# Fused attention and MLP on one core: batch 1's queries and keys loaded partly ahead of w_out, its scores started earlier, remainders and warm-up matmuls moved

## The chip, the cores and the metric

The kernel runs on one core of a Trainium2 chip. The core has five engines that run side by side and synchronise by semaphores: TensorE (PE in the profile; its weight loads are listed as PEld), VectorE (DVE), ScalarE (ACT), GpSimd (POOL) and SyncE (SP). Here GpSimd issues all loads, SyncE issues all stores and the transposing DMAs, and 16 DMA engines carry them all.

The metric is the device time of one execution in microseconds (us); the median of several runs is compared.

## The reference

Eight batches of causal attention with eight heads each, 576 positions and head size 64, with a decaying bias, are followed by a two-layer MLP with an exact GELU over all 4608 tokens:

```python
scores = scale * q @ k.T                          # per batch and head, 576 x 576
cum    = cumsum(maximum(s, 0))
scores = where(causal, -1e9, scores + minimum(-(cum_i - cum_j), 0))
attn   = softmax(scores)                          # with 1e-9 on the sum
x      = (attn @ v) as [4608 tokens, 512]
g      = gelu_exact(x @ w_in)                     # 512 -> 2048
out    = g @ w_out                                # 2048 -> 512, float32
```

## The kernel before, in words

**The attention.** One batch is treated as four pairs of heads (p = 0 to 3). For a pair, `sc_item` (L370) computes the scores with the key position on the partitions, in two units of up to 512 columns into PSUM tiles of the tag "sc" (two of them), and ScalarE takes the exponential into the tile P (L392, four buffers, one for each pair). `mask_item` (L398) zeroes the part above the diagonal on VectorE; for some pairs of batch 0 a matmul adds a large negative number instead (`neg=True`, L384). The decay is not added to the scores: each key position has a weight wb, v is multiplied by it once (`scale_v`, L225, L230, giving vv), and the numerator (lhsT = vv) and the denominator (lhsT = wb broadcast) come from two sets of matmuls (`av_mm`, L410, L414). `norm` (L427) takes the logarithm of the denominator and its negative exponential on ScalarE (L431, L432) and multiplies on VectorE into xT (L447), which is the MLP's input, transposed.

A batch has 576 positions and a PSUM bank holds 512 numbers of 4 bytes, so `av_item` (L452) does positions 0 to 511, and the last 64 positions of all four pairs, the remainder, share one bank (tile avr, `av_rest`, L467) and are normalised once (`norm_rest`, L473). Other than the "sc" tiles there are four PSUM banks: three of the tag "av", one of "mlp". An accumulator "wide" takes an "sc" tile.

**The MLP.** The 4608 tokens are cut into nine chunks of 512 (c). `l1_item` (L482) computes two of 16 tiles of the hidden layer (four matmuls of 128x128 by 128x512 for each, L495) and ScalarE applies GELU into gT (L501, L504). `l2_item` (L506) computes 128 tokens of the output (sub = 0 to 3) as 16 accumulating matmuls, ft = 0 to 15 (L514), which may be called in parts; after the last one VectorE copies the bank to o_sb (L521) and SyncE stores it (L523). Quarter i of w_out serves ft = 4i to 4i+3. A chunk's layer 1 has 64 matmuls, its layer 2 also 64.

**The order.** All engines follow the program's order (a manual schedule): each engine executes its own instructions in the order in which the program gives them, and waits where an operand or a buffer isn't ready. So the order of the calls in L563 to L719 is the plan. Batch 0's attention runs first (L563 to L600). In chunk c the layer 1 runs without other matmuls, and the attention of batch c+1 is mixed into its layer 2, since a chunk of 512 tokens needs the outputs of one batch more. Chunk 0 has its own order (L626 to L678), chunks 1 to 6 share one (L679 to L709).

Batches 0 and 1 have their q and k transposed on TensorE: `tr_item` (L353) does 18 small transposes into an "av" bank and a copy to qkT (L364; VectorE, or ScalarE where named). From batch 2 on, `interleave` (L174, L178) reorders on VectorE, `write_rows` (L185, L187) writes the rows to DRAM through SyncE's queue, and `transpose_rows` (L192, L194) reads them back with eight transposing DMAs, in the same queue.

**The loads.** GpSimd issues them in program order: first q, k and v of batch 0 and w_in, then, behind a small copy that waits for w_in's first quarter (`pace`, L593), the four quarters of w_out (L595, L247), q and k of batch 1 (`load_qk`, L596, four loads by `load_early`, L96, L101: the first q and k loads hold pairs 0 and 1, the second ones pairs 2 and 3), v of batch 1 (five loads, `load_v`, L196, L202) and q, k of batch 2. An issue waits when the load eight before it hasn't landed.

**Warm-up matmuls.** `keep_busy(n)` (L559, L561) issues n matmuls of 128x128 by 128x512 on zeros, whose result nobody reads.

**Side work.** `absmax` (L211) and `absmax_v` (L217) find the largest magnitudes for a check at the end, on VectorE, inside layer 1; when the check fails, a slow general version runs (from L724, not taken here).

Of the kernel before, what the change touches and what calls it, by code (L numbers as in the profile page):

```python
# [19 lines left out]
def kernel(  # L20
# [10 lines left out]
    nc = tc.nc  # L31
# [135 lines left out]
    def load_qk(b):  # L167
        for p in (0, 2):
            for n in "qk":
                load_early(b, n, p)  # L170
# [296 lines left out]
    def av_rest(b, p):  # L467
        if p == 0:
            rest_of[b] = ps.tile([128, 2, NP, SL], fp32, tag="av", bufs=3, name="avr")
        for den in range(2):  # L470
            av_mm(b, p, rest_of[b][:, den, p], [(jt, 0, n, off) for jt, n, off in REST], den)
# [87 lines left out]
    def keep_busy(n):  # L559
        for _ in range(n):  # L560
            nc.tensor.matmul(warm, lhsT=busy[:, :128], rhs=busy, start=True, stop=True)  # L561
# [10 lines left out]
    tr_item(0, 1, 1)  # L572
    nc.vector.tensor_scalar(neg_bf, tri_bf, 2048.0, -2048.0, op0=MULT, op1=ALU.add)
    weights_pe()
    keep_busy(2)
    sc_item(0, 1, neg=True)
    mask_item(0, 0, 0, nc.vector)
    mask_item(0, 0, 1, nc.vector)
    tr_item(0, 2, 0)
    tr_item(0, 2, 1)  # L580
    tr_item(0, 3, 0, nc.scalar.copy)
    tr_item(0, 3, 1)
    sc_item(0, 2, neg=True)
    keep_busy(1)
    sc_item(0, 3, neg=True)
    keep_busy(3)
    for st in range(ST - 1):
        scale_v(0, STS[st : st + 1], nc.vector)
    nc.vector.tensor_copy(uptri, tri_bf)
    nc.gpsimd.memset(amv, 0.0)  # L590
    nc.gpsimd.memset(ones, 1.0)
    nc.gpsimd.memset(qkT[1][:, 1, :, S:640], 0.0)
    nc.gpsimd.tensor_copy(pace, w_in_r[:, 0, 0:1])  # L593
    for i in range(4):
        load_w(1, i)  # L595
    load_qk(1)  # L596
    load_v(1)
    load_qk(2)
    for p in range(NP):
# [3 lines left out]
    for c in range(NCH):  # L603
# [9 lines left out]
            absmax_v(nb)  # L613
        if c == 0:
            absmax_v(0)
        if c < B:
            for p in range(NP):
                absmax(c, p)
# [7 lines left out]
        if c == 0:  # L626
            exp_set()
            load_v(2)
            l2_item(c, 0, av=True)
            scale_v(0, STS[ST - 1 :], nc.vector)  # L630
            for p in range(NP):
                av_rest(0, p)
            norm_rest(0)
            l2_item(c, 1, 0, 8)
            for p in (0, 1):
                for i in range(2):
                    tr_item(1, p, i)
            l2_item(c, 1, 8, 12)
            for i in range(2):
                tr_item(1, 2, i)  # L640
            l2_item(c, 1, 12)
            for i in range(2):
                tr_item(1, 3, i)
            sc_item(1, 0)
            l2_item(c, 2, 0, 6, av=True)
            sc_item(1, 1)
            l2_item(c, 2, 6, 12, av=True)
            scale_pair(1, 0)
            sc_item(1, 2)
            l2_item(c, 2, 12, av=True)  # L650
            sc_item(1, 3)
            scale_pair(1, 1)
            l2_item(c, 3, 0, 4)
            interleave(2, "q")
            write_rows(2, 0, nc.sync)
            av_item(1, 0, rest=False)
            scale_pair(1, 2)
            scale_pair(1, 3)
            l2_item(c, 3, 4, 8)
            interleave(2, "k")  # L660
            write_rows(2, 1, nc.sync)
            av_item(1, 1, wide=True, rest=False)
            l2_item(c, 3, 8, 12)
            for p in (0, 1):
                transpose_rows(2, p)
            av_rest(1, 0)
            av_rest(1, 1)
            av_item(1, 2, wide=True)
            l2_item(c, 3, 12)
            av_item(1, 3)  # L670
            norm_rest(1)
            gelu_set()
            for p in (2, 3):
                transpose_rows(2, p)
# [4 lines left out]
        elif nb < B:  # L679
            exp_set()  # L680
            l2_item(c, 0, 0, 4)
            sc_item(nb, 0)
            l2_item(c, 0, 4)
            late = int(c == 1)
            for p in range(1, NP):
# [185 lines left out]
```

## Time and profile before

| quantity | value |
|---|---|
| median of 5 runs | 333.86 us (333.38 to 335.44) |
| the profiled execution's own time | 333.19 us |
| span of the profile (first to last instruction) | 331.4 us |
| TensorE busy | 320.4 us, 97% of the span |
| VectorE, ScalarE, GpSimd busy | 193.4, 202.7, 65.0 us |
| TensorE's granted clock, mean | 0.997 |
| first layer-2 matmul of chunk 0 | 34.70 us |
| first layer-1 matmul of chunk 1 | 62.00 us |

How to read the profile: the page gives each engine's busy time, then the span in 40 slices of 8.3 us with a digit for the busy tenths of each. A line of a timeline or of the chain of waits has a start, a length, and the engine, line and tile of what ran; x16 means that 16 instructions are merged. In square brackets stands how long the engine had been idle just before, and, after the arrow, what ended that. Lengths of matmuls overlap, so the pace is read from the starts.

### The profile page before, as it was taken

The numbers are of one execution on the slowest core, as the hardware profiler recorded it, in microseconds if no ns is written. First come the engines' busy times: TensorE is split into PE (matmuls) and PEld (weight loads), VectorE is DVE, ScalarE is ACT, GpSimd is POOL, SyncE is SP. The second block draws the span as 40 slices with busy tenths as digits, with TensorE's granted clock in tenths as the row PEclk, the third lists the DMA queues.
The fourth block names the chain that finished last, engine by engine and source line by source line (L and its number), as shares of the span: only waits on it lengthen the run. The fifth ranks groups of instructions, "written<-read, shape, count | busy, mean of one in ns | idle before, by whom it ended". The sixth has DMA issues, their size and how long they took to land.

```text
span 331.4 us, 6416 instructions
## 1 busy us (share of the span) xinstructions
PE 320.4 (97%) x2590; PEld 163.8 (49%) x2590; DVE 193.4 (58%) x383; ACT 202.7 (61%) x288; POOL 65.0 (20%) x100
## 2 busy tenths in 40 slices
PE   8899899999999999999999999999999999999992
PEld 4554454545554455445544554455545544444452
DVE  6757187996569464947395657745693654150021
ACT  4886528868576766777576767677659566204400
POOL 8753351007000910620043002200000000000000
PEclk9999999999999999999999999999999999999998
DMA  7999999777965999899779465626600110010012
GB/s 121 222 211 208 219 228 242 203 135 110 276 199 132 156 227 267 171 199 270 156 145 206 139 189 127 138 105 166 132 15 32 45 53 2 32 63 32 3 63 71
DMA packets 53828, 47.30 MB, mean 143 GB/s; under 512 B 31328, under 2 KB 43872, under 8 KB 53792
## 3 DMA queue, kind: packets, MB, share of 16 engines
q0 software_dynamic: 15936, 23.07, 37.7%
q1 hardware_dynamic: 37856, 23.75, 27.0%
q8 instruction: 22, 0.36, 0.4%
q14 instruction: 14, 0.11, 0.1%
HBM read 36.85 MB, written 16.52 MB: 161 GB/s over the span
## 4 chain that ended last, share of the span: by engine, by line
PE 94%; ACT 3%; DVE 2%; issue 0%
PE h_ps L495 38%; PE o_ps L514 37%; PE sc_ps L376 5%; PE avn L414 4%; PE avd L414 3%; ACT P L392 2%; PE warm L561 2%; PE tr_ps L359 1%; PE avr L414 1%; PE o_ps L533 1%; DVE qkT L364 1%; PE avw L414 1%; PE sc_ps L384 0%; ACT ln L432 0%; ACT ln L431 0%
## 5 line engine op out<-in xcount | busy, mean ns | idle before, releaser
L514 PE MATMUL o_ps<-w_out_r,gT 128*128 128x512 bf16 x560 | 129.7, 380 | 0.0
L495 PE MATMUL h_ps<-xT,w_in_r 128*128 128x512 bf16 x576 | 126.0, 379 | 0.7 <-DVE xT L447 0.7
L495 PEld LDWEIGHTS <-w_in_r 128*128 128x128 bf16 x576 | 56.2, 98 | 68.7 <-issue 1.4
L501 ACT ACTIVATE gT<-h_ps 128x1024 bf16<-128x1024 f32 x54 | 54.3, 1022 | 48.8 <-PE h_ps L495 48.8
L392 ACT ACTIVATE P<-sc_ps 128x1024 bf16<-128x1024 f32 x64 | 61.9, 1021 | 33.8 <-PE sc_ps L376 32.2
L514 PEld LDWEIGHTS <-gT 128*128 128x128 bf16 x560 | 51.4, 98 | 58.6
L521 DVE COPY o_sb<-o_ps 128x512 f32<-128x512 f32 x35 | 24.1, 688 | 53.0 <-PE o_ps L514 53.0
L401 DVE TENSOR_TENSOR P<-P,tri_bf 128x512 bf16<-128x512 bf16 x58 | 24.3, 424 | 38.8 <-ACT P L392 38.6
L213 DVE TENSOR_REDUCE amx<-qkT 128x2 f32<-128x1152 bf16 x32 | 40.9, 1335 | 0.0
L447 DVE SCALAR_TENSOR_TENSOR xT<-avn,ln 128x256 bf16<-128x256 f32 (+3 forms) x64 | 21.7, 385 | 25.9 <-ACT ln L432 25.9
L202 POOL DMA_DIRECT2D raw_v<-in_v_dram x40 | 34.3, 882 | 10.1 <-DMA w_out_r<-in_moe_w_out_dram 6.5
L230 DVE TENSOR_TENSOR vv<-raw_v,wb 128x512 bf16<-128x512 f32 (+2 forms) x43 | 25.4, 644 | 0.9 <-DMA raw_v<-in_v_dram 0.9
L431 ACT ACTIVATE ln<-avd 128x256 f32<-128x256 f32 x56 | 18.6, 391 | 11.2 <-PE avd L414 11.2
L432 ACT ACTIVATE ln<-ln 128x512 f32<-128x512 f32 (+1 forms) x40 | 23.5, 587 | 1.3
L220 DVE TENSOR_REDUCE amv<-raw_v 128x1 f32<-128x2048 f32 (+1 forms) x16 | 23.0, 1470 | 1.4 <-DMA raw_v<-in_v_dram 1.4
L504 ACT ACTIVATE gT<-h_ps 128x512 bf16<-128x512 f32 x36 | 19.6, 603 | 6.3 <-PE h_ps L495 6.3
L376 PE MATMUL sc_ps<-qkT 64*128 64x256 bf16 (+2 forms) x320 | 21.5, 250 | 1.3 <-ACT P L392 0.9
L376 PEld LDWEIGHTS <-qkT 64*128 64x128 bf16 x320 | 13.2, 94 | 16.8 <-issue 14.2
L414 PEld LDWEIGHTS <-vv 128*64 128x64 bf16 x384 | 16.8, 109 | 8.3 <-issue 3.8
L414 PEld LDWEIGHTS <-wb 128*64 128x64 bf16 x384 | 17.0, 111 | 0.0
L414 PE MATMUL avn<-P,vv 128*64 128x256 bf16 x224 | 16.0, 265 | 0.0
L414 PE MATMUL avd<-P,wb 128*64 128x256 bf16 x224 | 15.4, 259 | 0.0
(94 smaller groups left out, 159.6 us busy)
## 6 DMA issues: line engine op xcount, KB each, us to landing
out_dram<-o_sb SPq DMA_DIRECT2D x35, 256.0 KB, 2.3
raw_v<-in_v_dram POOLq DMA_DIRECT2D x32, 256.0 KB, 7.4
rows<-qk_bf SPq DMA_DIRECT2D x12, 576.0 KB, 3.8
early_q<-in_q_dram POOLq DMA_DIRECT2D x14, 288.0 KB, 9.2
early_k<-in_k_dram POOLq DMA_DIRECT2D x14, 288.0 KB, 9.3
w_in_r<-in_moe_w_in_dram POOLq DMA_DIRECT2D x4, 512.0 KB, 11.0
w_out_r<-in_moe_w_out_dram POOLq DMA_DIRECT2D x4, 512.0 KB, 12.9
raw_v<-in_v_dram POOLq DMA_DIRECT2D x8, 128.0 KB, 9.3
```

Of the source, the lines that this page charges most:

```text
L202: nc.gpsimd.dma_start(out=t[:n_st, st, :, :], in_=bass.AP(tensor=v.tensor, offset=v.offset + b * H * S * D + st * 128 * D, ap=[[D, n_st], ...
L213: nc.vector.tensor_reduce(amx[:, b * NP + p], qkT[b % 2][:, :, p, :S], axis=AX, op=ALU.max, apply_absolute_value=True)
L230: eng.tensor_tensor(vb[:n_st, st0:st1, h0:h1, :], t[:n_st, st0:st1, h0:h1, :], wb[:n_st, st0:st1, b * H + h0 : b * H + h1] .unsqueeze(3).t ...
L376: nc.tensor.matmul(s_ps[:, e, off : off + n], lhsT=qkT[b % 2][e * 64 : e * 64 + 64, 1, p, jt * 128 : jt * 128 + 128], rhs=qkT[b % 2][e * 6 ...
L392: nc.scalar.activation(P[:, :, UO[u] : UO[u] + UW[u]], s_ps[:, :, : UW[u]], func=AF.Exp, scale=scale)
L401: eng.tensor_tensor(d, d, tri_bf.unsqueeze(1).unsqueeze(1).to_broadcast([128, 2, 2, 128]), op=MULT)
L414: nc.tensor.matmul(out[e * 64 : e * 64 + 64, lo : lo + n], lhsT=(wb[:, jt, b * H + h : b * H + h + 1].to_broadcast([128, 64]) if den else ...
L432: nc.scalar.activation(ln[:, :w], ln[:, :w], func=AF.Exp, scale=-1.0)
L495: nc.tensor.matmul(h_of[c, f2][i], lhsT=w_in_r[:, ko, ft * 128 : (ft + 1) * 128], rhs=xT[:, ko, c * NB % XW : c * NB % XW + NB], start=(ko ...
L501: nc.scalar.activation(gT_of[c][:, f2 * 2 : f2 * 2 + 2, :], hh_of[c, f2], func=AF.Gelu)
L514: nc.tensor.matmul(o_ps, lhsT=gT[:, ft, sub * 128 : (sub + 1) * 128], rhs=w_out_r[:, ft, :], start=(ft == 0), stop=(ft == FT - 1),)
L521: nc.vector.tensor_copy(o_sb, o_ps)
```

## The change

It has seven parts.

1. Batch 0's opening: `tr_item(0, 2, 0)` takes the place of `keep_busy(2)` ahead of the second pair's scores, and `tr_item(0, 2, 1)` stands ahead of the masks instead of behind them. `keep_busy(3)` behind the last scores is gone.
2. The scaling of v's fourth slice (positions 384 to 511) of batch 0 is cut into two halves of four heads.
3. The scaling of v's last slice (positions 512 to 575) of batch 0 is issued in chunk 0's layer 1, behind `absmax_v(0)` and ahead of `absmax`, instead of behind item 0 of layer 2.
4. The loads of the first halves of q and k of batch 1 are issued ahead of w_out's four quarters, the second halves behind them.
5. Layer 2 of chunk 0 opens with batch 0's remainder and the first transposes of batch 1, and every item of it is cut in two halves of 8 matmuls with transposes, scores and outputs of batch 1 in between. Items 0 and 2 and 3 use the "mlp" bank, item 1 an "av" bank (before: 0 and 2 "av", 1 and 3 "mlp").
6. Batch 1's remainder and its normalisation leave chunk 0's layer 2 and go into chunk 1's, ahead of and behind the first scores of batch 2.
7. All eight transposing DMAs of batch 2 now stand behind both writes of rows and the fourth store.

```diff
     weights_pe()
-    keep_busy(2)
+    tr_item(0, 2, 0)
     sc_item(0, 1, neg=True)
+    tr_item(0, 2, 1)
     mask_item(0, 0, 0, nc.vector)
     mask_item(0, 0, 1, nc.vector)
-    tr_item(0, 2, 0)
-    tr_item(0, 2, 1)
...
     sc_item(0, 3, neg=True)
-    keep_busy(3)
-    for st in range(ST - 1):
+    for st in range(ST - 2):
         scale_v(0, STS[st : st + 1], nc.vector)
+    for h in (0, H // 2):
+        scale_v(0, STS[ST - 2 : ST - 1], nc.vector, h, h + H // 2)
...
+    for n in "qk":
+        load_early(1, n, 0)
     for i in range(4):
         load_w(1, i)
-    load_qk(1)
+    for n in "qk":
+        load_early(1, n, 2)
     load_v(1)
     load_qk(2)
...
             absmax_v(0)
+            scale_v(0, STS[ST - 1 :], nc.vector)
...
             load_v(2)
-            l2_item(c, 0, av=True)
-            scale_v(0, STS[ST - 1 :], nc.vector)
             for p in range(NP):
                 av_rest(0, p)
+            tr_item(1, 0, 0)
+            tr_item(1, 0, 1)
+            l2_item(c, 0, 0, 8)
+            tr_item(1, 1, 0)
+            tr_item(1, 1, 1)
             norm_rest(0)
-            l2_item(c, 1, 0, 8)
-            for p in (0, 1):
-                for i in range(2):
-                    tr_item(1, p, i)
-            l2_item(c, 1, 8, 12)
-            for i in range(2):
-                tr_item(1, 2, i)
-            l2_item(c, 1, 12)
-            for i in range(2):
-                tr_item(1, 3, i)
             sc_item(1, 0)
-            l2_item(c, 2, 0, 6, av=True)
+            l2_item(c, 0, 8)
             sc_item(1, 1)
-            l2_item(c, 2, 6, 12, av=True)
+            l2_item(c, 1, 0, 8, av=True)
+            tr_item(1, 2, 0)
+            tr_item(1, 2, 1)
+            l2_item(c, 1, 8, av=True)
+            tr_item(1, 3, 0)
+            tr_item(1, 3, 1)
             scale_pair(1, 0)
             sc_item(1, 2)
-            l2_item(c, 2, 12, av=True)
+            l2_item(c, 2, 0, 8)
+            scale_pair(1, 1)
             sc_item(1, 3)
-            scale_pair(1, 1)
-            l2_item(c, 3, 0, 4)
+            l2_item(c, 2, 8)
+            scale_pair(1, 2)
+            av_item(1, 0, rest=False)
+            scale_pair(1, 3)
+            av_item(1, 1, wide=True, rest=False)
+            l2_item(c, 3, 0, 8)
             interleave(2, "q")
             write_rows(2, 0, nc.sync)
-            av_item(1, 0, rest=False)
-            scale_pair(1, 2)
-            scale_pair(1, 3)
-            l2_item(c, 3, 4, 8)
+            av_item(1, 2, wide=True, rest=False)
+            l2_item(c, 3, 8)
             interleave(2, "k")
             write_rows(2, 1, nc.sync)
-            av_item(1, 1, wide=True, rest=False)
-            l2_item(c, 3, 8, 12)
+            av_item(1, 3, rest=False)
             for p in (0, 1):
                 transpose_rows(2, p)
-            av_rest(1, 0)
-            av_rest(1, 1)
-            av_item(1, 2, wide=True)
-            l2_item(c, 3, 12)
-            av_item(1, 3)
-            norm_rest(1)
             gelu_set()
...
             l2_item(c, 0, 0, 4)
+            if c == 1:
+                for p in range(NP):
+                    av_rest(1, p)
             sc_item(nb, 0)
+            if c == 1:
+                norm_rest(1)
             l2_item(c, 0, 4)
```

## The prediction

> **What bounds the kernel now.** I read the page's busy shares first, then TensorE's waits, then the chain of waits from the start to the second chunk (0 to 62 us), then the same stretch engine by engine, with the issues of GpSimd's queue.
>
> ```profile
> PE 320.4 (97%) x2590; PEld 163.8 (49%) x2590; DVE 193.4 (58%) x383; ACT 202.7 (61%) x288; POOL 65.0 (20%) x100
> DMA  7999999777965999899779465626600110010012
> ...
> PE avr L414 <- DVE vv L230: 1.2, 1, 1.2
> PE sc_ps L376 <- ACT P L392: 0.9, 3, 0.5
> ```
>
> TensorE is the bound: only its work or its waits can be shortened, 11 us of idle at most. The DMA engines are as full in the first 50 us (the first six slices, 8.3 us each) and free later. From chunk 1 on the chain is TensorE without a gap, so everything is decided before 62 us. There TensorE runs:
>
> ```profile
> 1.20 3.60 PE warm L561 x8
> ...
> 16.13 0.65 PE warm L561 x3
> 16.77 0.91 PE avw L414 x16
> 17.70 0.67 ACT ln L431 x2
> ...
> 34.87 3.47 PE o_ps L514 x16
> 38.36 0.69 DVE o_sb L521
> 39.05 0.60 DVE vv L230
> 39.69 0.66 PE avr L414 x30
> 40.36 1.83 PE o_ps L514 x8
> ...
> 43.92 0.97 PE o_ps L514 x4
> 44.89 0.69 PE tr_ps L359 x36
> ```
>
> The columns are start, length, work. A layer-2 matmul costs 3.47/16 = 0.217 us in a long group, but 4 of them cost 0.97 and 8 cost 1.83: each seam adds about 0.1. The remainder (avr) waits 1.2 us, because vv's last rows are scaled behind o_sb on VectorE. Which loads come when is seen where GpSimd stands still (start, length of the issue, and the load whose landing ended the idle time):
>
> ```profile
> 29.20 0.91 POOL L202 DMA_DIRECT2D raw_v<-in_v_dram  x1 [1.29 <-DMA w_out_r<-in_moe_w_out_dram]
> 37.14 0.88 POOL L202 DMA_DIRECT2D raw_v<-in_v_dram  x1 [1.92 <-DMA w_out_r<-in_moe_w_out_dram]
> 38.55 0.69 POOL L202 DMA_DIRECT2D raw_v<-in_v_dram  x1 [0.54 <-DMA early_q<-in_q_dram]
> 39.98 0.63 POOL L101 DMA_DIRECT2D early_q<-in_q_dram  x1 [0.73 <-DMA early_k<-in_k_dram]
> ```
>
> So w_out's quarters are in by 29.2 to 37.1, the first halves of q and k of batch 1 by 38.5 and 39.9. Issue times plus landing times in the DMA view give the rest: second halves by 41.8 and 43.3, v of batch 1 by 48.6 (37.14 + 11.5) with its last piece at 49.45 (38.55 + 10.9).
>
> **The head (to 21 us).** Five warm-up matmuls go (5 x 0.217 = 1.1 us of TensorE), but they filled waits. What counts is when the first denominators of batch 0 reach ScalarE, 17.70 before. TensorE then came to av only at 16.70, after three warm-ups. Now it stands ready and waits for v's fourth slice, which VectorE scaled at 16.08 to 16.78 (two in 1.40 from 15.38). Cut in halves, the first is done by about 16.5 (0.4, between the 0.28 of a 64x128 and the 0.68 of a 128x512). Two short matmuls and the denominators (0.55) follow: 17.15, so ln starts at 17.2. ScalarE's exponentials ended at 17.19 even unmoved, and start up to 0.9 earlier, since batch 0's third pair is copied ahead of the masks. Gain 0.5; bounds 0 (v lands later) and 0.65 (the three warm-ups). The first layer-2 stage opens at 34.2 instead of 34.7. The transposes put in front of the second scores need q that landed at 4.07 + 4.3 = 8.4; they start at 8.7, in the cover of the earlier copies (to 9.14).
>
> **Loads past each other.** Two issues (0.6 us each on GpSimd) go ahead of four of w_out (3.0 together); these land 10 to 16 us after issue, so issue is covered. Bytes ahead of the v loads are unchanged. q, k first halves now land around 28 and 29.5, w_out's last three quarters around 34.5, 37.1 and 39.8: its last quarter takes the place in line that k had (39.7 to 40.0).
>
> **The stage from 34.2 on**, in the new order, durations from the rows above (tr pair 0.69, sc 0.54, av 0.89, eight layer-2 matmuls 1.83, remainder 0.62). Remainder to 34.8: its v slice is scaled right after absmax_v (28.3), so the 1.2 wait is gone; 0.67 is added ahead of the absmax, which ends at 33.4 and holds nobody. Transposes to 35.5; half of item 0 to 37.3; transposes to 38.0; scores 0 to 38.6. Item 0's second half would want the last quarter of w_out at 39.43: a new wait of 0.4 (bounds: 0 if it lands at 37.1 as before; 2.4 if it only lands with the next in line, second q, 41.8; I take k's old place, as the bytes ahead are the same as k's were). Item 0 ends 40.9, scores 1 41.5, half of item 1 43.3, transposes 44.0 (k lands at 43.3, covered by the q transposes), item 1 45.8, transposes 46.5, scores 2 47.1, half of item 2 48.9, scores 3 49.4, item 2 51.3, av 0 52.2, av 1 53.0.
>
> VectorE has little cover here. It reaches the scaling of v of batch 1 at 47.9 and stands until 48.65 and 49.45 (before, it came at 51.99 and found v there). Behind it in its queue are masks 2, scaling 1, masks 3 and the eviction of item 2: 0.3 + 1.0 + 0.88 + 1.0 + 0.68 brings 53.3. Item 3 uses the one "mlp" bank and waits for that eviction: from 53.03 to 53.35, 0.3 us. Bounds: none if v is there at 47.9, and one 256 KB transfer more (44.3, 45.5, 46.75, 48.65: about 1.3 us each) if an output store lies differently. I take the old landing, as the line in front of v is the same. Then item 3's half 55.2, av 2 56.1, item 3 57.9, av 3 58.8. Its xT is ready at 60.9 (ScalarE 1.3, VectorE 0.75, with the second interleave ahead ending at 59.7); chunk 1 wants it at 58.8 + 12 x 0.217 = 61.4. Chunk 1 opens at 58.8 instead of 62.0: 3.2 earlier.
>
> **What is given back.** Batch 1's remainder (0.62 plus a seam, 0.7) and its normalisation (ScalarE 0.8, VectorE 0.42) go into chunk 1's layer 2. There ScalarE is busy 3.48 of 4 us and VectorE 2.35 (80 to 84 us) and TensorE never waited; masks lead their av by over 2 us, so the two small ones are covered, at worst 0.4. SP now has the fourth store and the second rows ahead of all eight transposes; rows follow the interleaves, which end at 57.3 and 59.7 instead of 57.6 and 60.7, and the transposes (12 us, before done by 76.1) are first wanted at 74.2, for pair 0, ready by about 67 (rows 4 us, the first two transposes 3). The loads of batch 3 behind them landed by 86.8 and fed an interleave at 86.0 and 91.1; the first needs 84.2 and would now run at 83.5, a VectorE wait of 0.7 with 2.7 of lead to av.
>
> **Sum.** The stage takes 24.6 us (34.2 to 58.8) for 27.3 (34.7 to 62.0), 2.7 less: remainder's wait 1.2, deferred remainder 0.6, three seams fewer 0.3, short waits that the new order lacks 1.25 (0.45 before the fourth transposes at 43.45, 0.5 before scores 3 at 53.74, 0.3 in scores that took 0.87 for 0.54), less 0.7 of new waits. With 0.5 of the head that is the 3.2; less 0.7 given back it is 2.5. The profiled execution took 333.19 (span 331.4 and 1.8 around it), 0.67 below the median of the runs, 333.86. Taken from the span, 328.9; from the execution 330.7; carried to the median, 331.3.
>
> **Weighing the clock.** The page grants full clock throughout (0.997), yet the first eight matmuls took 3.60, 450 ns each against 217 later: there is a half-rate start. From 42.1 to 45.5 the trace has 108 transposes and only 4 layer-2 matmuls, and the next four layer-2 matmuls still took 0.97, as the others do: transposes did not slow it there, and I charge nothing. The Trainium skill (TensorE: Matmul & The Clock Gate, Part 4: PE-mode transpose) says that transposes don't count as TensorE's work for the clock, which speaks against replacing warm-ups by them; by its window of 3.4 us at half rate the sum would be 1.7 worse, about 333.0.
>
> **The rivals.**
> 1. The loads decide. v or w_out lands late by one or two 256 KB pieces, VectorE's wait runs straight into item 3: 1 us late costs 1 us, as cover is nil. For it: DMA is full to 50 us, and both new waits stand on landings I moved or met earlier. Against: the same bytes, in the same line. Price 1.3: gain 1.2, 332.6.
> 2. Slower: the clock falls after the warm-ups go. From 13.05 to 16.5 TensorE would work only 1.8 of 3.4 us (before, 3.7 of 4.1 us from 12.6). A cold stretch of t us loses t/2: 3.6 us as at the start loses 1.8 (333.1); it decides from 5 us; if layer 1 of chunk 0 ran cold to its middle (7 us) 3.5 are lost: 334.8. Against: from 36.5 to 39.9 it worked 2.18 of 3.40 us and the next matmuls ran at 229 ns.
> 3. The change gives nothing: the head's 0.5 vanishes in the w_out wait anyway, and a wait as long as the remainder's 1.2 comes back in chunk 1, because "av" has three banks and the remainder holds one through scores 0: gain 2.5 - 0.5 - 1.2 = 0.8, 333.0. Against: avr is issued before the scores and the av that needs three banks comes 3 us later.
>
> **How the numbers follow.** Forecast 0.64 (330.3 to 332.2, its own range); loads late 0.15; nothing 0.09; clock 0.12, half of it slower. About 0.5% (1.7 us) is what a measurement of this kernel can tell from no change, so faster means below 332.2. Faster 0.66 (forecast, and a little of the loads' case), same 0.23, slower 0.11. Range 330.2 to 333.8: at the low end neither landing binds (0.7 more) and the runs lie 0.4 lower, about as the lowest of before (333.38) under its median; at the high end one cold stretch (333.1) and 0.7, the distance of the profiled execution from the median.
>
> **What would show it.** Right: avr's wait gone; chunk 1's first h_ps near 58.8; w_out's wait on TensorE under 1 us near 39.5; VectorE standing for raw_v near 48 to 49.5; the first h_ps group ending near 34.2; warm x2 fewer and x3 fewer. Wrong: layer-1 groups of chunk 0 above 14 us (clock), chunk 1's layer 2 longer than 21.5 (20.75 before plus 0.7), or item 3 starting after 54.

## The result, and the profile after

The changed kernel takes 331.98 us (median of 42 runs, 330.84 to 335.22) against 333.86 for the kernel before (median of 79). The ratio is 0.9942, with a 95% interval of 0.9928 to 0.9956: 1.9 us or 0.6% less. The profiled execution took 331.8 us, its span is 330.0 (before 333.19 and 331.4). In the experiments, runs more than 1.5% above the fastest of their kernel count as a slower state and are left out of medians and ratios (one each of c4, d1 and of before beside c and d, two of before beside e).

First the page's engine shares and DMA row of the changed kernel, busy tenths in slices of 8.3 us:

```profile
PE 320.8 (97%) x2585; PEld 164.2 (50%) x2585; DVE 193.2 (59%) x384; ACT 202.8 (61%) x288; POOL 65.5 (20%) x100
DMA  7999999846986899999679676425500100010012
```

Then TensorE's waits of the changed kernel (what waited, for what, us in total, times, longest):

```profile
PE sc_ps L376 <- ACT P L392: 0.7, 3, 0.3
PE h_ps L495 <- DVE xT L447: 0.6, 1, 0.6
PE avd L414 <- DVE xT L447: 0.3, 1, 0.3
```

The remainder's wait of 1.2 us is gone from the list, as forecast, and nothing of its size has come. But a new line has appeared, avd waiting for xT, and it isn't in the stage that was changed. Where the time went is seen from the first matmul of each layer 1 (TensorE's timeline; times in us; in chunk 0 a single matmul stands about 1 us ahead, and the row gives the one from which layer 1 runs on; layer 2 of chunk 0 opens with item 0 before and with the remainder after):

| | before | forecast | after |
|---|---|---|---|
| layer 1 of chunk 0 | 21.07 | 20.57 | 21.69 |
| layer 2 of chunk 0 | 34.70 | 34.2 | 35.42 |
| chunk 1 | 62.00 | 58.8 | 59.35 |
| chunk 2 | 96.56 | 94.06 | 94.52 |
| chunk 3 | 131.12 | 128.62 | 129.62 |
| length of chunk 1 / chunk 2 | 34.56 / 34.56 | 35.26 / 34.56 | 35.17 / 35.10 |

Chunk 1 opened 2.65 us earlier than before, chunk 3 only 1.50. The chain of waits of the changed kernel tells what set the first of these times (start, length, work):

```profile
23.97 16.95 DMA w_out_r<-in_moe_w_out_dram
40.92 0.04 issue
40.96 1.02 PE o_ps L514 x4
...
58.53 0.50 PE avn L414 x8
59.03 0.38 PE avd L414 x8
59.42 4.64 PE h_ps L495 x21
```

A load stands in the chain where there was only engine work before: w_out's last quarter, landed at 40.92, starts the last four matmuls of item 0, and from there TensorE goes without a gap for 18.4 us to chunk 1 (59.35). So chunk 1 opens 18.4 us after that landing, as long as TensorE has come to those four matmuls by then. Here it had come only just before: the half of item 0 took 2.19 us for the 1.90 of the others, so the wait is about 0.3. Further on, the same view of the changed kernel leaves TensorE a second time:

```profile
94.69 10.36 PE h_ps L495 x48
...
105.10 2.94 DMA qkT<-rows
...
108.71 0.65 POOL early_q L101
...
109.95 6.66 DMA early_q<-in_q_dram
...
116.80 0.55 DVE qk_bf L178 x2
...
117.69 0.59 DVE P L401 x2
...
118.57 0.68 DVE xT L447 x2
119.25 0.04 issue
119.29 0.57 PE avd L414 x8
```

Read from top to bottom this is a second chain: the transposing DMAs of batch 3 end, GpSimd's pace copy lets the loads of batch 4 go, q of batch 4 lands, VectorE reorders it, and only then come to their turn on VectorE the masks and xT, for which TensorE waits. The view of the kernel before is TensorE alone from 62 us on. VectorE's timeline of the changed kernel shows its three waits for loads:

```profile
49.74 0.89 DVE L230 TENSOR_TENSOR vv<-raw_v,wb 128x512 bf16<-128x512 f32 x2 [0.80 <-DMA raw_v<-in_v_dram]
86.90 0.83 DVE L178 COPY qk_bf<-early_q 128x1152 bf16<-128x1152 bf16 x2 [2.98 <-DMA early_q<-in_q_dram]
116.80 0.98 DVE L178 COPY qk_bf<-early_q 128x1152 bf16<-128x1152 bf16 x2 [2.73 <-DMA early_q<-in_q_dram]
```

Before, the last two ran at 86.02 and 116.02 with no wait. GpSimd's timeline gives the reason; here the pace copies of the kernel before:

```profile
76.08 0.18 POOL L675 CAST pace<-qkT 128x1 f32<-128x1 bf16 x1 [24.34 <-DMA qkT<-rows]
107.09 0.18 POOL L699 CAST pace<-qkT 128x1 f32<-128x1 bf16 x1 [23.77 <-DVE amx L213]
```

and of the changed one:

```profile
77.09 0.21 POOL L673 CAST pace<-qkT 128x1 f32<-128x1 bf16 x1 [24.11 <-DMA qkT<-rows]
108.18 0.19 POOL L702 CAST pace<-qkT 128x1 f32<-128x1 bf16 x1 [23.84 <-DMA qkT<-rows]
```

TensorE came 2 to 2.7 us earlier, while this chain came 1.0 and 1.1 later. (The second line of before names VectorE's absmax, the last of several waits to end; the eight transposing DMAs ahead of it were issued from 94.02 on before and from 94.91 on after.) For batch 3 the load itself took longer too: the second half of q needed 8.0 us from issue to landing, 6.4 before (DMA times of early_q), so it landed at 86.85 instead of 84.2. The leads of before, 1.8 us for batch 3 and 0.8 for batch 4, had been enough; now they are used up. Chunk 2 is 0.54 longer for it (avd waits 0.35 and then takes 0.57 for its usual 0.38), chunk 1 about 0.15 (there the same matmuls, at 89.35, take 0.54 for 0.38). From chunk 3 on the loads are let go earlier, by a pace copy on gT, and chunk 3 again lasts 34.56 in both kernels.

### The profile page after: what moved, and what is told of

Its sections match the earlier page's. It is cut to its first block, busy times and chain, and to the rows that moved or that the text cites. A ratio compares the mean times of both kernels' runs of the same rounds, so it can differ in the third digit from the quotient of the medians.

```text
span 330.0 us, 6402 instructions
## 1 busy us (share of the span) xinstructions
PE 320.8 (97%) x2585; PEld 164.2 (50%) x2585; DVE 193.2 (59%) x384; ACT 202.8 (61%) x288; POOL 65.5 (20%) x100
## 4 chain that ended last, share of the span: by engine, by line
PE 81%; DMA 12%; POOL 3%; DVE 1%; issue 1%; DVEq 0%; POOLq 0%
PE o_ps L514 35%; PE h_ps L495 32%; DMA w_out_r<-in_moe_w_out_dram 5%; PE sc_ps L376 4%; PE avn L414 4%; DMA w_in_r<-in_moe_w_in_dram 4%; PE avd L414 3%; DMA early_q<-in_q_dram 2%; PE o_ps L533 1%; POOL raw_v L202 1%; PE avr L414 1%; DMA qkT<-rows 1%; POOL early_k L115 1%; POOL early_q L115 1%; PE avw L414 1%
## 5 line engine op out<-in xcount | busy, mean ns | idle before, releaser
L230 DVE TENSOR_TENSOR vv<-raw_v,wb 128x512 bf16<-128x512 f32 (+3 forms) x44 | 25.2, 633 | 0.8 <-DMA raw_v<-in_v_dram 0.8
```

The source lines that it names most:

```text
L230: eng.tensor_tensor(vb[:n_st, st0:st1, h0:h1, :], t[:n_st, st0:st1, h0:h1, :], wb[:n_st, st0:st1, b * H + h0 : b * H + h1] .unsqueeze(3).t ...
```

## The experiments

Kernels whose labels share a letter ran on the same chip beside the kernel before; the ratio is to those runs. It isn't the quotient of the two medians and is smaller than it in every run but d1, most of all in the e group (e4: 0.9925, quotient 0.9976), where runs of before reach up to 338.21 us. So kernels of one group are best compared with each other by their medians. Where no word is said, a number is from the profile of the kernel named.

| run | median us (runs) | before beside it | ratio, 95% interval | w_out's last quarter noticed at | chunk 1 | chunk 1's length | chunk 2's length | chunk 3 |
|---|---|---|---|---|---|---|---|---|
| c1_changed_again | 332.13 (10) | 333.93 | 0.9925, 0.9893 to 0.9957 | 40.94 | 62.15 | 35.02 | 34.55 | 131.72 |
| c2_rows_early | 331.89 (12) | 333.93 | 0.9927, 0.9896 to 0.9958 | 42.84 | 62.57 | 35.02 | 34.56 | 132.15 |
| c3_busy3_back | 332.74 (12) | 333.93 | 0.9957, 0.9924 to 0.9990 | 41.33 | 59.47 | 35.90 | 34.86 | 130.23 |
| c4_no_late_warm | 332.66 (11) | 333.93 | 0.9944, 0.9918 to 0.9970 | 41.13 | 61.44 | 35.02 | 34.56 | 131.02 |
| d1_pace_early | 332.30 (11) | 333.93 | 0.9957, 0.9925 to 0.9989 | 42.17 | 60.32 | 35.02 | 34.56 | 129.90 |
| d2_swap | 332.43 (12) | 333.93 | 0.9926, 0.9898 to 0.9954 | 41.06 | 59.04 | 36.39 | 35.27 | 130.70 |
| d3_pace_swap | 332.34 (12) | 333.93 | 0.9932, 0.9900 to 0.9963 | 41.46 | 59.75 | 35.92 | 34.55 | 130.22 |
| d4_slice_early | 332.57 (12) | 333.93 | 0.9949, 0.9927 to 0.9971 | 36.92 | 60.55 | 34.57 | 34.56 | 129.68 |
| e1_wout_first | 334.65 (10) | 333.87 | 0.9995, 0.9952 to 1.0037 | 37.18 | 62.52 | 35.02 | 34.56 | 132.10 |
| e2_rest_back | 331.96 (12) | 333.87 | 0.9919, 0.9882 to 0.9956 | 42.04 | 60.69 | 34.56 | 34.56 | 129.81 |
| e3_slice_head | 331.76 (12) | 333.87 | 0.9922, 0.9883 to 0.9960 | 37.66 | 60.82 | 34.57 | 34.56 | 129.95 |
| e4_other_order | 333.08 (12) | 333.87 | 0.9925, 0.9886 to 0.9964 | 37.53 | 61.74 | 35.02 | 34.56 | 131.32 |

("Noticed" is the start of the GpSimd issue that waited for it; the landing is up to 0.3 earlier.)

### The changed kernel once more

> The changed kernel itself, beside which the three others of this group are read. Expected 0.994 of the kernel before (331.9 for 333.9). What is open is how the gain divides. In the two profiles chunk 1 opens 2.65 us earlier, chunk 2 2.04 earlier, chunk 3 only 1.50 earlier. If the long cold start in the changed kernel's profile (small transposes of the opening at 0.69 us for 18 until 8.5 us, before 0.47 from 5.3 on) is chance, this profile should show a first av group at about 16.5 to 17.3 and a wait of about 1 us for w_out's last quarter near 40.9; if the change causes it, the long start is there again.

The time came back, 332.13. But the profile fell on an execution of 334.06 us that is unlike the first one in its opening. TensorE's timeline of this run:

```profile
8.37 0.69 PE L359 MATMUL tr_ps<-ident_bf,early_q 64*64 64x64 bf16 x18
13.76 0.69 PE L359 MATMUL tr_ps<-ident_bf,early_k 64*64 64x64 bf16 x18
```

Eighteen transposes take 0.69 us at the half rate of the start and 0.47 at the full one. In the kernel before they were at 0.47 from 5.3 us, in the changed kernel's first profile from 9.65, here not before 20. The windows of the same run (the columns are the stretch, its length, the busy time of PE, PEld, DVE, ACT and POOL, each with its count of instructions, then granted clock, DMA share and GB/s) show neither idleness nor a lower granted clock:

```profile
12.00:16.00 4.00, 4.00 (x73) 2.62 (x72) 1.86 (x6) 2.69 (x3) 2.65 (x6) 1.00 1.08 211
```

Layer 1 started at 24.78, 3.1 later than in the first profile, and chunk 3 opened 2.1 later: a late opening meets loads that have landed meanwhile, and gets part of it back.

Of the two cases in the expectation: that the half rate outlasts 8 us isn't the change's doing. In after the half rate ended by 9.65 us, ahead of the first TensorE instruction that the change put elsewhere (the transposes at 10.49), and in c1 the transposes at 8.37 were already slow; up to there both kernels give TensorE the same instructions. Whether the change makes it last to 20 us stays open.

### Batch 2's rows written earlier

```diff
             write_rows(2, 0, nc.sync)
-            av_item(1, 2, wide=True, rest=False)
-            l2_item(c, 3, 8)
             interleave(2, "k")
             write_rows(2, 1, nc.sync)
+            av_item(1, 2, wide=True, rest=False)
+            l2_item(c, 3, 8)
```

> The changed kernel with the second rows of batch 2 (k) interleaved and written right behind the first (q), two steps earlier, so that the transposing DMAs of batch 2 start about 1.3 us earlier (62.4 as in the kernel before, instead of 63.7). Theory: the 0.54 us lost in chunk 2 come from a second chain, transposes of batch 2, then the loads of batch 3, its interleave and rows, its transposes, then the loads of batch 4, which VectorE awaits for 2.7 us in chunk 2; that chain starts later in the changed kernel though TensorE is earlier. Expected: pace copies at about 75.8 and 107 instead of 77.1 and 108.2, VectorE's wait for q of batch 4 under 1.6, chunk 2 34.6 long instead of 35.1, 0.4 to 0.55 us faster than the changed kernel. Rival: chunk 2 is long for another reason (clock or banks): no change.

It isn't a clean test, because TensorE was 3 us late in this profile, and the median, 331.89 beside 332.13 of the changed kernel, can't be told from it. The second rows were issued on SyncE's queue right behind the first (60.80, two in 1.11 us), and yet the transposing DMAs started at 64.30, 2.4 us behind them, and the pace copy at 77.67. In the kernels with the new layer 2 they began between 62.9 and 64.6, with the old one between 62.0 and 62.4. Two things hold them. Where TensorE came late (c1, c4, e1, e4) they were issued about 0.5 us behind the second rows: there it is the order in the queue. Elsewhere they wait for the first rows to land: in after these were issued at 57.58 and the transposing DMAs at 63.70, 6.1 later; before, at 57.67 and 62.40, 4.7 later. SyncE's waits name the rows, first in after, then before (the whole run: us in total, times, longest):

```profile
SPq L194 <- DMA rows<-qk_bf: 23.8, 10, 5.8
SPq L194 <- DMA rows<-qk_bf: 17.5, 10, 6.0
```

Why TensorE was late is in its own timeline:

```profile
42.60 1.85 PE L514 MATMUL o_ps<-w_out_r,gT 128*128 128x512 bf16 x4 [2.63 <-DMA w_out_r<-in_moe_w_out_dram]
```

w_out's last quarter landed at 42.56, and after that wait of 2.63 us the four matmuls took 1.85 instead of 1.02. The windows of the same run show the granted clock falling:

```profile
42.00:44.00 2.00, 1.40 (x4) 0.40 (x3) 0.00 (x0) 0.00 (x0) 0.63 (x1) 0.66 1.10 176
44.00:46.00 2.00, 2.00 (x14) 0.86 (x13) 0.69 (x1) 0.96 (x2) 0.86 (x2) 0.50 1.04 221
46.00:48.00 2.00, 2.00 (x37) 0.97 (x37) 0.98 (x3) 0.97 (x2) 1.04 (x3) 0.98 1.07 200
```

From the landing to chunk 1 it took 20.0 us instead of 18.4: 1.6 on top of the wait. Waits of 1.48 (d1) and 1.77 (e2) at the same place left the clock at 1.00.

### Three warm-up matmuls back

```diff
     sc_item(0, 3, neg=True)
+    keep_busy(3)
     for st in range(ST - 2):
```

> The changed kernel with the three warm-up matmuls ahead of batch 0's first av put back, nothing else. If the head's step of the forecast holds (0.5 us saved, of which the wait for w_out gives back a part), this is 0 to 0.5 us slower than the changed kernel, with layer 1 of chunk 0 opening up to 0.5 later and w_out's wait shorter by as much. If the missing warm-ups cost clock, this one is faster than the changed kernel by 1 us or more.

No gain and no loss that can be told: 332.74, and its interval covers the changed kernel's ratio. The profile repeats the second chain, with a wait of 3.71 us for q of batch 3 and chunk 1 at 35.9. In the chain of waits of this run it is the line

```profile
79.63 8.04 DMA early_q<-in_q_dram
```

### The other late warm-up matmuls taken out

```diff
     weights_dve()
-    keep_busy(3)
     sc_item(0, 0, masks=False)
     tr_item(0, 1, 0)
-    keep_busy(1)
     tr_item(0, 1, 1)
...
     sc_item(0, 2, neg=True)
-    keep_busy(1)
     sc_item(0, 3, neg=True)
```

> The changed kernel without any warm-up matmul behind the first eight (the remaining 3 + 1 + 1 go, 1.1 us of TensorE). Rival of the clock: TensorE drops to half pace or stays there longer, matmuls of layer 1 in chunk 0 at 0.43 us instead of 0.216 for some us, 1.8 us slower or more. Theory that warm-ups only fill waits: within 0.4 us of the changed kernel, since q, k and v land when they land.

The time, 332.66, can't be told from that of the changed kernel. The profile, of an execution of 333.41 us, has the half rate until about 20 us (layer 1 at 24.08), as c1 has with these warm-ups in place. So removing warm-ups doesn't by itself decide it, and whether it makes the very long opening more frequent is open. The half rate passed 7.5 us in five of the twelve profiles with the new opening (to about 9.5 in after and e4, to 20 in c1, c4 and e1) and in neither of the two with the old one (before, d4), which are too few. Of the changed kernel's 42 runs 31 lie at 332.43 and below, ten between 333.5 and 334.4 and one at 335.22, with nothing between; but of c1's ten runs of the same kernel two, 333.15 and 333.32, lie in that gap. The upper group may be the long opening (the profile of c1 is one of 334.06), but these runs have no profile. The kernel before has a slow tail too, up to 338.4.

### The pace copies wait for less

```diff
-            nc.gpsimd.tensor_copy(pace, qkT[0][:, 1, 3, 0:1])
+            nc.gpsimd.tensor_copy(pace, qkT[0][:, 1, 1, 0:1])
...
-                        nc.gpsimd.tensor_copy(pace, qkT[(nb + 1) % 2][:, 1, p, 0:1])
+                        nc.gpsimd.tensor_copy(pace, qkT[(nb + 1) % 2][:, 1, 1, 0:1])
```

> The changed kernel with one edit: the small copies that let the loads of batches 3 and 4 (q, k) start wait for the transposed k of pair 1 instead of pair 3, that is about 6 us earlier (near 71 and 102 instead of 77 and 108). Theory of the second chain (transposes, loads, interleave, rows): VectorE's waits for q of batch 3 (2.98 us at 86.9) and of batch 4 (2.73 at 116.8) go or shrink below 1, chunk 1 is 35.1 long and chunk 2 34.55 instead of 35.09, and the time is 0.5 to 0.7 us under the changed kernel's. Rival: the loads then run beside the transposing DMAs, which take longer (over 14 us for eight instead of 11.3 to 12.9), and nothing is gained.

This tells the second chain from the deferred remainder. The pace copies ran 4 to 6 us earlier (GpSimd's timeline), and VectorE's reordering found its data (VectorE's timeline, no bracket):

```profile
72.89 0.18 POOL L673 CAST pace<-qkT 128x1 f32<-128x1 bf16 x1 [19.33 <-DMA qkT<-rows]
102.47 0.18 POOL L702 CAST pace<-qkT 128x1 f32<-128x1 bf16 x1 [22.34 <-DMA qkT<-rows]
```

```profile
84.80 0.82 DVE L178 COPY qk_bf<-early_q 128x1152 bf16<-128x1152 bf16 x2
114.80 0.84 DVE L178 COPY qk_bf<-early_q 128x1152 bf16<-128x1152 bf16 x2
```

Chunk 2 fell back to 34.56 and chunk 1 to 35.02: the loads' chain cost 0.54 and 0.15, the deferred remainder and its normalisation cost 0.46. But the gain of 0.5 to 0.7 that was expected didn't come: 332.30. In this profile w_out's last quarter came later (a wait of 1.48) and chunk 1 opened at 60.32; whether that took the gain in the other runs too isn't shown.

### Items 0 and 1 exchanged

```diff
-            l2_item(c, 0, 8)
-            sc_item(1, 1)
-            l2_item(c, 1, 0, 8, av=True)
+            l2_item(c, 1, 0, 8, av=True)
+            sc_item(1, 1)
+            l2_item(c, 0, 8)
```

> The changed kernel with the second half of item 0 of chunk 0's layer 2 (which needs the last quarter of w_out) exchanged with the first half of item 1 (which needs only the first two). The last quarter lands at 40.7 to 42.6 in the five profiles, 0.9 to 2.8 us later than the 39.8 of the forecast, and TensorE waited for it 0.3 us (39.8 on), 0.5 and 2.6 us where its opening was fast. Theory: that wait eats the head's saving. Expected: no wait for w_out, chunk 1 opens up to 2.6 us earlier where the opening is fast, 0.3 to 1.0 us in the median, unless VectorE's wait for v of batch 1 (49.5) takes its place, ahead of item 3. Rival: the median is set by other waits, no change within 0.3.

Item 0's second half, which needs w_out's last quarters, now stands behind item 1's first half, and the wait for w_out is gone. Chunk 1 opened at 59.04, the earliest of all. Chunk 3 opened at 130.70, later than in any other run of the table whose opening was short and whose clock stayed up. The chain of waits of this run runs through two other loads:

```profile
35.17 14.28 DMA raw_v<-in_v_dram
59.11 0.75 PE h_ps L495 x3
...
80.04 7.69 DMA early_q<-in_q_dram
...
90.22 0.57 PE avd L414 x8
```

Everything was given back, and the median is 332.43: VectorE waited 4.20 us for q of batch 3 and 2.91 for that of batch 4.

### Both edits

```diff
-            l2_item(c, 0, 8)
-            sc_item(1, 1)
-            l2_item(c, 1, 0, 8, av=True)
+            l2_item(c, 1, 0, 8, av=True)
+            sc_item(1, 1)
+            l2_item(c, 0, 8)
...
-            nc.gpsimd.tensor_copy(pace, qkT[0][:, 1, 3, 0:1])
+            nc.gpsimd.tensor_copy(pace, qkT[0][:, 1, 1, 0:1])
...
-                        nc.gpsimd.tensor_copy(pace, qkT[(nb + 1) % 2][:, 1, p, 0:1])
+                        nc.gpsimd.tensor_copy(pace, qkT[(nb + 1) % 2][:, 1, 1, 0:1])
```

> Both edits together. If the two waits are separate and each is on the path, the gains add: 0.8 to 1.5 us under the changed kernel. If the w_out wait only hides the second chain's, the exchange alone gives nothing and the two together more than the sum.

With w_out's wait and the loads' wait both out of the way, the next link came up. Scores of batch 2 wait 0.82 us at 89.53 for a transposing DMA itself, which the chain of waits of this run follows back for 14.46 us:

```profile
75.02 14.46 DMA qkT<-rows
```

Chunk 1 is again 35.92 long, and the median, 332.34, is no better. The loads now run beside the transposing DMAs. In the three runs with early pace copies the slowest of the eight took 13.0 (d1), 14.5 (d3) and 10.6 us (e4) from issue to landing; in the other profiles it took at most 5.0, in after 4.1.

### The slice of v alone, on the kernel before

```diff
         if c == 0:
             absmax_v(0)
+            scale_v(0, STS[ST - 1 :], nc.vector)
...
             l2_item(c, 0, av=True)
-            scale_v(0, STS[ST - 1 :], nc.vector)
             for p in range(NP):
                 av_rest(0, p)
```

> The kernel before with one part of the change alone: v's last slice of batch 0 scaled inside layer 1 of chunk 0. Theory: the 1.2 us wait ahead of the remainder goes, TensorE reaches the transposes 1.2 earlier at 40.9, but there q and k of batch 1 landed only at 38.5 and 39.9, so they are in; the later waits for exponentials stay. Expected 0.8 to 1.2 us faster than the kernel before. Rival: the loads of batch 1 (k's second half at 43.3 to 43.6) take it back, under 0.5.

Part 3 of the change, two lines, gives 1.36 us (333.93 to 332.57), a little above the 0.8 to 1.2 expected, and its interval and the whole change's overlap. The chain of waits shows the remainder directly behind item 0, with engine work alone on the chain:

```profile
34.84 3.45 PE o_ps L514 x16
38.29 0.62 PE avr L414 x32
```

The chain of loads came earlier with TensorE here (pace copies at 75.23 and 105.92, no wait on VectorE), since the rows and transposes kept their places.

### w_out's loads first again

```diff
-    for n in "qk":
-        load_early(1, n, 0)
     for i in range(4):
         load_w(1, i)
-    for n in "qk":
-        load_early(1, n, 2)
+    load_qk(1)
```

> The changed kernel with the loads in their old order (all of w_out ahead of batch 1's q and k), the new order of work kept. TensorE comes to the first transposes of batch 1 near 35 to 36, and q and k landed at 38.5 and 39.9 in that order: a wait of 3 to 4 us ahead of or inside them, item 0 then without a wait for w_out (in by 37.1). Chunk 1 opens near 61.5 to 62.5 instead of 59.0 to 60.3, time 1.5 to 2.5 above the changed kernel's if nothing hides it. Rival: what is lost here was going to be lost in the second chain anyway (chunk 1 then shows 34.6 to 35.1 and no wait for batch 3's loads), and the time is less than 1 us above.

Without part 4 the new layer 2 loses the whole gain: 334.65 beside 333.87 of before, ratio 0.9995; that is 2.7 above e2 below, which is the changed kernel but for its part 6, on the same chip. The chain of waits of this run goes through batch 1's k:

```profile
24.72 15.03 DMA early_k<-in_k_dram
```

It landed at 39.75. TensorE waited only 0.31 us for it, because this execution had the long half-rate opening; the 3 to 4 us expected behind a short opening are in no profile. So the early loads are what the new order needs, and the changed kernel pays for them with a later w_out.

### The remainder of batch 1 back in chunk 0

```diff
-            av_item(1, 3, rest=False)
+            for p in range(NP - 1):
+                av_rest(1, p)
+            av_item(1, 3)
+            norm_rest(1)
...
             l2_item(c, 0, 0, 4)
-            if c == 1:
-                for p in range(NP):
-                    av_rest(1, p)
             sc_item(nb, 0)
-            if c == 1:
-                norm_rest(1)
```

> The changed kernel with batch 1's remainder and its normalisation back at the end of chunk 0's layer 2 and out of chunk 1's. Chunk 1 opens 0.6 later (60 to 61), is 34.6 long by its own work, and VectorE's wait for batch 3's q is about as much shorter. Time within 0.4 us of the changed kernel's, if anything lower, since the remainder's 0.6 us now lie ahead of the point where the second chain binds. If the move was worth its 0.6, it is 0.6 slower.

331.96: moving the remainder (part 6) is neutral. Chunk 1 opens later by about as much as it is shorter, 34.56 again. VectorE's waits for batches 3 and 4 were 2.00 and 1.43, and cost TensorE nothing: the loads' chain binds only when TensorE comes early.

### Parts 1 to 3 on the kernel before

```diff
-    keep_busy(2)
+    tr_item(0, 2, 0)
     sc_item(0, 1, neg=True)
+    tr_item(0, 2, 1)
...
-    keep_busy(3)
-    for st in range(ST - 1):
+    for st in range(ST - 2):
         scale_v(0, STS[st : st + 1], nc.vector)
+    for h in (0, H // 2):
+        scale_v(0, STS[ST - 2 : ST - 1], nc.vector, h, h + H // 2)
...
             absmax_v(0)
+            scale_v(0, STS[ST - 1 :], nc.vector)
...
             l2_item(c, 0, av=True)
-            scale_v(0, STS[ST - 1 :], nc.vector)
```

> The kernel before with three parts of the change only: v's last slice scaled inside layer 1 (1.4 us faster by itself), the reordered opening without the five warm-ups, and the fourth slice in halves. The loads are in the old order, so no wait for w_out's last quarter beyond 0.3 us. If the head's step is right, layer 1 opens at 20.5 to 20.7 where the opening is fast and the time is 0.3 to 0.5 below that kernel's, 332.1, level with the whole change. Rival: the head's saving ends in waits for q and k of batch 1, 332.5 or above.

The opening's edits and the slice, with the old loads and the old layer 2, are level with the whole change: 331.76, beside 331.96 of e2 on the same chip and 331.98 of the changed kernel; the intervals of the ratios overlap. Parts 4 to 7, the bulk of the diff, bring nothing that can be measured beyond these; with intervals of 0.4% to either side, a difference of less than about 1 us wouldn't be seen. The head's gain is seen when each profile is measured from the landing of w_in, at which GpSimd's first pace copy runs (GpSimd's timeline of this run):

```profile
19.28 0.19 POOL L593 CAST pace<-w_in_r 128x1 f32<-128x1 bf16 x1 [3.31 <-DMA w_in_r<-in_moe_w_in_dram]
```

Layer 1 follows it at 21.31, by 2.03. In the six other profiles with the new opening and a short half-rate stretch it is 2.03 to 2.13 (c2, c3, d1, d2, d3, e2); with the old opening it is 2.58 (before: 18.49 to 21.07) and 2.50 (d4). About 0.45 us, at equal landing times. c3, with 2.11, has the three warm-up matmuls back, so their going isn't shown to be what gave it; there they filled a wait for v.

### Another order, with w_out first

```diff
             for p in range(NP):
                 av_rest(0, p)
+            norm_rest(0)
+            l2_item(c, 0)
+            l2_item(c, 1, 0, 8, av=True)
             tr_item(1, 0, 0)
             tr_item(1, 0, 1)
-            l2_item(c, 0, 0, 8)
             tr_item(1, 1, 0)
             tr_item(1, 1, 1)
-            norm_rest(0)
             sc_item(1, 0)
-            l2_item(c, 0, 8)
+            l2_item(c, 1, 8, av=True)
             sc_item(1, 1)
...
```

with w_out's loads first, as in e1_wout_first, the pace copies as in d1_pace_early, and the transposes of pairs 2 and 3 around item 2's first half.

> An attempt at a better version from these readings: w_out first as before, but layer 2 of chunk 0 opens with the remainder, all of item 0 and half of item 1, so that TensorE comes to batch 1's transposes only at 40, when q and k are in; and the loads of batches 3 and 4 start behind pair 1's transposes as in the run with earlier pace copies. No wait for w_out, none for q and k, chunk 1 opens at 58.8 to 59.5 and is 35.1 long: 0.5 to 1.2 us under the changed kernel, 330.9 to 331.6. Rival: v of batch 1 (in by 49.5 to 50.5) or the transposing DMAs beside the loads take it back, within 0.4 of the changed kernel.

It doesn't beat the changed kernel: 333.08, 1.1 above e2, and chunk 1 opened at 61.74 for the 58.8 to 59.5 expected. Its opening ran at half rate until 9.5 us, as in after. Four short waits for copies of transposes (0.57, 0.20, 0.15, 0.20) and one of 1.23 for the scaling of v of batch 1 came (TensorE's timeline):

```profile
54.61 0.57 PE L414 MATMUL avn<-P,vv 128*64 128x256 bf16 x8 [1.23 <-DVE vv L230]
```

## Why the prediction was right, and where it was not

The prediction, 331.3 us, was 0.7 too low, and the direction and most of the mechanism were right. From the profiled executions, 331.8 measured and 330.7 forecast, it was 1.1 too low; 0.5 of that was made good by luck, because the forecast was carried to the median with 0.67, the distance of the one profiled execution of before, and after's profiled execution lies only 0.18 under its median.

Luck is in the division too. By the sum, parts 1 to 3 were worth 1.7 (the remainder's wait 1.2 and the head 0.5), and parts 4 to 7 another 0.75 (deferred remainder 0.6, seams 0.3, short waits 1.25, less 0.7 of new waits and 0.7 given back). Measured, parts 1 to 3 alone give 2.1 (333.87 to 331.76) and the rest nothing that can be told. The new order did open chunk 1 earlier, at 59.35 in after for 60.82 in e3, but behind it most was given back: chunk 3 opened at 129.62 and 129.95.

**The remainder's wait: right.** Its 1.2 us were there to be had by two moved lines, and d4_slice_early measures 1.36 for them alone.

**The head: right in itself, lost behind it.** Forecast 0.5, measured 0.45 at equal landing times; which of its edits gave it isn't shown (c3). In the changed kernel it didn't reach the end. In the first profile after, the half rate lasted longer and layer 1 started at 21.69 for the forecast 20.57. And where the opening was short, w_out's landing took it: from then on only that landing counted (18.4 us to chunk 1 in after, c3 and d1).

**w_out's last quarter: the term that was mis-sized.** The sum had it land at 39.8, in the place that k had before, for a wait of 0.4. It landed at 40.92 in after and up to 42.56 in c2, 1.1 to 2.8 later. With the opening as late as in after, TensorE waited 0.3; with a short one it waited 1.48 (d1) and 1.77 (e2), inside the bound of 2.4, and 2.63 in c2, outside. Counting the same bytes ahead of a load gave its place in the line, but not its time. The issue of that quarter was also held, until 23.97 (all four had left by 21.72 before), though the forecast had taken issue as covered; but the third quarter, whose issue wasn't held, was noticed 3.6 later as well (37.95 for 34.34), so that explains little.

**The stage from 34.2 on: right, a little shorter than worked out.** From the landing to chunk 1 the forecast has 19.0 us (39.8 to 58.8), after had 18.4 (40.92 to 59.35). Item 3's forecast wait of 0.3 didn't come: v of batch 1 landed at 49.7, VectorE stood 0.80, and item 3 started at 53.91 with no wait. There TensorE came 0.9 later than forecast, and so was late for it; where it came earlier the wait was there: item 3 waited 0.16 (d2) and 0.65 (d3) for the eviction of item 2, with VectorE standing 1.16 and 1.83 for v.

**Given back in chunk 1: right in size, by two terms for one.** Forecast 0.7, all of it the remainder and its normalisation; measured 0.61, of which these are 0.46 and the loads' chain 0.15.

**The loads of batches 3 and 4: the step that failed.** "A VectorE wait of 0.7 with 2.7 of lead to av" was 2.98 us, and batch 4's loads in chunk 2 weren't in the sum at all; they cost 0.54. The step took the loads' old landing, 84.2, and moved only TensorE. VectorE was ready at 83.9, as forecast, but q landed at 86.85. The loads hang on the transposing DMAs, these on the rows, and that chain came 1.0 later where it had to come earlier; the other 1.6 is the load's own time, 8.0 for 6.4.

The four deviations of the profiled execution's chunk 3 from the forecast add up: w_out's last quarter 1.12 later, the rest of chunk 0 0.57 shorter, chunk 1 0.09 shorter, chunk 2 0.54 longer, 1.00 together (129.62 for 128.62).

**The rivals.** The first, that loads decide (332.6), was right on the mechanism, and at a lower price: loads stand on the chain of after at two places, but not at v, where it was looked for most (there only in d2). Shifted orders only choose which load it is: w_out and batch 4's q in after, v and batch 3's q in d2, the transposing DMAs in d3. The second, the clock, isn't the median's story: putting warm-ups back (c3) or taking more out (c4) moved it by nothing that can be told. But its price was right where it struck single executions: layer 1 at 24.78 and 334.06 us in c1, where the forecast had 333.1 to 334.8. The third, a gain of 0.8 (a ratio of 0.9976), lies outside the interval.

What is shown: part 3 gives most of the gain, part 4 is needed by part 5, part 6 is neutral, and parts 4 to 7 together add nothing measurable to parts 1 to 3. What is only argued: that the rows land later in the new order, and the transposing DMAs behind them, because rows, loads and stores share full DMA engines until about 64 us (their share is 1.04 from 60 to 62 us and 0.94 from 62 to 64 in after; before, 0.43 and 0.72). No run took those transfers away.

## What to carry to other kernels

When one engine is pulled earlier, ask for each chain that feeds it whether that chain moves with it. Here load, reorder, write, transposing DMA and next load form a ring paced by DMA, whose slack of 1.8 us (batch 3) and 0.8 us (batch 4) didn't show before, since VectorE never waited for those loads.

The lead of a load over its user isn't shown by a profile in which the user never waits; take it from the landing, not from the user's start. A few moved lines that remove one measured wait on the bound engine (part 3) were worth as much as a reordering of the whole stage around it.

## What the runs showed of the hardware

**The half rate of the opening has no fixed length.** Nearly the same instructions ran at half rate until 5 to 7 us (before, c2, c3, d1 to d4, e2, e3), 9.5 us (after, e4) and 20 us (c1, c4, e1), with TensorE busy 15.2 of the 16 us from 4 to 20 in c1. The granted clock in the profile read 1.00 throughout, so here the length of a known group tells the rate and the clock column doesn't. The Trainium skill (TensorE: Matmul & The Clock Gate, Part 1, What's actually happening) has the full rate come after one busy window of about 3.4 us. The shortest openings (TensorE starts at 1.20 and is at full rate near 5) roughly agree with it, the 20 us of c1 don't.

**A wait in the middle can bring the half rate back.** After 2.63 us without work the granted clock in c2 was 0.66, 0.50 and 0.98 in the next three windows of 2 us, and 1.6 us were lost beside the wait. After waits of 1.48 and 1.77 nothing fell. The same section gives about 3.4 us of idling as what lowers the rate; the wait here was shorter.

**A load put behind two others was delayed by more than their time.** The first halves of q and k, 288 KB each, were noticed 2.8 us behind w_out's last quarter before (39.98 for 37.14). When they went ahead of w_out's quarters, the last quarter was noticed 3.8 to 5.7 us later than before (between 40.94 and 42.84), with 1.9 us of difference between executions of nearly the same order; with the old order it lay between 36.92 and 37.66 in five profiles. The forecast had 2.7.

**Loads beside a transposing DMA delay its landing.** The slowest of the eight of batch 2 took at most 5.0 us from issue to landing in eleven profiles, and 10.6 to 14.5 in the three in which the loads of batch 3 were let go before the eight were done (d1, d3, e4).
